# One list of steps in place of three for an mLSTM and two mixture layers on one core

## The chip, the cores and the metric

The kernel runs on one core of a Trainium2 chip. Times are device microseconds of one execution, from three runs of the kernel before; the trace comes from one further, profiled execution. Lower is better. The engines are named as in the profile: PE (TensorE), with its weight loads as PEld, DVE (VectorE), ACT (ScalarE), POOL (GpSimd) and SP (SyncE, which here only issues DMAs).

## The reference

An mLSTM recurrence over 4 batches, 8 heads, 768 positions and 40 channels feeds a dense layer with a softmax in it, and that feeds a layer in which each of the 3,072 tokens goes to one of 8 experts. Shapes: x is 3072 x 320, d_ff is 1024.

```python
for t in range(S):
    m_new = np.maximum(f_gate[:, :, t] + m, i_gate[:, :, t])
    C = f_stab * C + i_stab * outer(vt, kt); n = f_stab * n + i_stab * kt
    y[:, :, t] = sigmoid(o_gate) * (C @ qt) / np.maximum(np.abs(n . qt), 1.0)
h = x @ w_in; e = exp(h - max(h)); solu = h * e / sum(e)
x = (solu - mean) / sqrt(var + 1e-6) * g_ln @ w_out
e_idx = argmax(x @ w_gate + modality_bias[modality_id])
out[mask] = gate_w[mask, None] * (relu(x[mask] @ w1[e]) @ w2[e])
```

## The kernel before, in words

The tokens are 24 tiles of 128: tile n is batch n % 4, chunk n // 4. Work is written as small functions, here called steps, each with a tile number or the like. A list of steps in text is read by `_steps` (line 49), and `play` (line 1193) calls them in that order. Each engine has one queue, which it works through in order; what is left open is where each step's instructions stand in it. For an engine that is named to `play` the queue is the order of the list (line 1196). For the others a planner, which knows the instructions' dependencies and its own costs, lays out the queues when the program is built, and the list only says what comes first when two are free.

The steps, by what they do for a tile n:

- Loads, all on SP's queue: `load_kv` (q and k transposed, k, v; lines 261 to 270), `load_a` (line 272: the running sums of the gates, broadcast to 128 x 1024; tile "abc", three buffers), `load_ea` (line 279, three buffers), `load_sig` (line 292: 128 x 6 x 320 floats of output gates for six tiles).
- The recurrence, by chunks: `decay` (line 544, two operations on POOL) and `decay_exp` (line 553, ACT) make the decay matrix in place in "abc"; for the first four tiles `decay_mm` and `decay_exp0` do so from PE. `k_t` and `k_e` (lines 515, 522) transpose k on PE and copy it out on ACT; `score` (line 574) is q times k on PE; `pmul` (line 583, two halves on DVE) multiplies by "abc", which is its last reader but for `scale_v`. `mix_x` (line 595, PE) applies the scores and the state; `mix_e` (line 608) copies out; `mix_c` (line 615, PE and DVE) adds to the state; `scale_q`, `scale_v` and `decay_c` are POOL's. `norm_t` (line 634) transposes back on PE, `norm_d` (line 641) makes the denominator with one operation on ACT, two on DVE and one on POOL ("sig"), `norm_x` (line 650, DVE) multiplies. `k_t`, `norm_t` and `mix_c` write one and the same PSUM buffer, tag "tr", of which there is one.
- The dense layer: `xs_p`, `xs_e` (lines 661, 669) transpose x and split it; `ff_mm` (line 679, two halves of eight matmuls on PE) fills one PSUM tile "h" (one buffer); `ff_max` (DVE), `ff_exp` (ACT), `ff_u` (DVE, the last reader of "h"), `ff_sq` (ACT), `ff_r` (DVE, four small ones), `ff_y` (ACT, and a transposing DMA on SP), `ff_yl` (DVE, and another), lines 691 to 734; `proj` (line 739, 24 matmuls) and `rows` (line 750: ACT, DVE, and a DMA of the row on SP).
- Its weights: `w_raw` (line 378, a DMA on ACT's queue into one of two buffers), `w_dec` (line 384: a square on ACT, four operations on DVE), `w_in_h`, `w_in_l`, and the `wo_` steps (lines 415 to 492), which must end before `proj` 0.
- The routing: `r1a`, `r1b`, `r2`, `r3` (lines 776 to 862) for groups of 7, 7, 4, 4 and 2 tiles; `table_a`, `table_w`, `table_get`, `table_b` (lines 896 to 1007) make the lists of tokens of each expert.
- The experts, in units j of 256 or 128 tokens of one expert: `fetch_w` (line 1009: an indirect DMA on POOL's queue, 128 x 3072 floats or 128 x 2560), `fetch_x`, `stat_a` (ACT), `stat_d` (DVE), `scale` (a small matmul, then DVE), `s1h`, `s1l`, `s2h`, `s2l` (the weights split into two halves of 16 bit), `h` (line 1108, PE), `hh`, `hl`, `po` (line 1154, PE), `ob` (ACT, and an indirect DMA).

Some steps do nothing for some tiles: `mix_c` and `scale_v` for the last four, `scale_q`, `load_ea` and `decay_c` for the first four (lines 559, 567, 591, 617).

Before the change there are three lists. PROLOGUE and STEADY are played with no engine named; TAIL names ACT and SP (line 1202). PROLOGUE goes to `ff_mm` 1 and `proj` 0, STEADY to the end of the recurrence and `proj` 18, TAIL through the first units of the experts, up to `po` 2. Behind it `units` runs the other units from the lists PAIR, HALF and so on, with PE, ACT and DVE named; there are 14 units in all in this input, two of them halves.

Of the kernel before, what the change touches and what calls it, by code (L numbers as in the profile page):

```python
# [54 lines left out]
PROLOGUE = _steps("""  # L55
    gates_m 0 128, c_pad, load_kv 0, gates_a 0 128, gates_c 0 128, load_kv 1, load_kv 2, scale_q 0, k_t 0, load_kv 3,
    c_route, k_e 0, w_raw 0, decay_mm 0, score 0, load_kv 4, k_t 1, decay_exp0 0, load_sig 0, decay_mm 1,
    w_dec 0, scale_v 0, w_in_h 0, k_e 1, w_raw 1, c_row, pmul 0 0, w_dec 1, w_raw 2, decay_exp0 1, do_sig 0,
    pmul 0 1, scale_q 1, w_in_l 0, w_in_h 1, score 1, k_t 2, w_in_l 1, w_dec 2, w_in_h 2, decay_mm 2,
    scale_v 1, gates_m 128 768, gates_a 128 768, k_e 2, c_ids, gates_c 128 768, w_raw 3, w_in_l 2,  # L60
    gates_e 128 768, w_dec 3, g_close, mix_x 0, w_in_h 3, load_ea 4, load_kv 5, pmul 1 0, decay_exp0 2,
    scale_v 2, mix_c 0, wo_open, mix_e 0, norm_t 0, pmul 1 1, w_raw 4, scale_q 2, decay_c 0, k_t 3, norm_d 0,
    decay_mm 3, k_e 3, w_dec 4, score 2, w_in_l 3, decay_c 1, pmul 2 0, decay_c 2, load_a 4, load_kv 6,
    load_kv 7, norm_x 0, mix_x 1, score 3, decay_exp0 3, load_a 5, w_in_h 4, pmul 2 1, mix_c 1, mix_e 1,
    decay 4, scale_v 3, mix_x 2, norm_t 1, decay_exp 4, norm_d 1, k_t 4, decay_c 3, decay 5, load_ea 6, k_e 4,
    w_raw 5, xs_p 0, w_dec 5, scale_v 4, scale_q 3, mix_c 2, score 4, norm_x 1, w_in_h 5, w_in_l 4, pmul 3 0,
    mix_e 2, pmul 3 1, w_in_l 5, norm_t 2, mix_x 3, norm_d 2, mix_e 3, xs_e 0, k_t 5, k_e 5, w_raw 6, mix_c 3,
    score 5, load_kv 8, pmul 4 0, norm_x 2, load_kv 9, load_ea 5, scale_q 4, ff_mm 0 0, w_raw 7, decay_exp 5,
    load_sig 1, load_a 6, norm_t 3, norm_d 3, pmul 4 1, k_t 6, w_dec 6, decay 6, mix_x 4, wo_t 0, load_ea 7,
    norm_x 3, pmul 5 0, mix_e 4, k_e 6, pmul 5 1, wo_g 0, decay_exp 6, w_dec 7, wo_s 0, wo_t 1, scale_v 5,  # L70
    wo_t 2, ff_mm 0 1, ff_max 0, scale_v 6, load_a 7, scale_q 5, ff_exp 0, ff_u 0, mix_x 5, decay_c 4, wo_s 1,
    wo_g 1, w_raw 8, xs_p 1, ff_sq 0, mix_c 4, w_raw 9, ff_r 0, ff_y 0, wo_g 2, score 6, w_dec 8, decay_c 5,
    xs_e 1, wo_s 2, norm_t 4, pmul 6 0, load_kv 10, decay 7, norm_d 4, wo_t 3, scale_q 6, decay_exp 7, mix_e 5,
    k_t 7, w_dec 9, pmul 6 1, wo_g 3, norm_x 4, mix_c 5, wo_t 4, wo_s 3, k_e 7, load_a 8, w_raw 10, wo_s 4,
    wo_g 4, score 7, wo_t 5, w_dec 10, wo_g 5, wo_s 5, wo_t 6, wo_t 7, wo_s 6, wo_g 7, prep_bias, wo_g 6,
    wo_s 7, wo_m, wo_c 2, wo_c 0, load_ea 8, wo_c 3, ff_yl 0, xs_p 2, decay 8, ff_mm 1 0, norm_t 5, wo_c 1,
    wo_c 4, wo_n, ff_mm 1 1, ff_max 1, ff_exp 1, ff_u 1, ff_sq 1, wo_f 1, ff_r 1, ff_y 1, wo_f 0, wo_f 2,
    wo_close, decay_c 6, do_sig 1, load_a 9, k_t 8, k_e 8, pmul 7 0, mix_x 6, mix_e 6, mix_c 6, load_kv 11,
    norm_d 5, scale_v 7, decay_exp 8, proj 0, pmul 7 1, scale_q 7, load_ea 9, norm_x 5, xs_e 2
""")  # L80
# [1222 lines left out]
```

## Time and profile before

| | us |
|---|---|
| median of 3 runs | 716.49 |
| lowest, highest | 708.62, 721.01 |
| the profiled execution: its time, its span | 718.84, 717.0 |
| busy in the span: PE, PEld | 568.4, 434.7 |
| busy in the span: DVE, ACT, POOL | 498.5, 372.0, 359.5 |

The span goes from the first to the last instruction. A busy share is an average over all stages; matmuls overlap in the pipeline, and their ends are modelled, so that PE's share is read together with its idle time and its clock. The clock that the chip granted to PE is a share of 2.4 GHz: 1.00 is that, 0.50 is 1.2 GHz. Its mean over the span is 0.895. A wait names what ended it; the chain of waits follows from the last instruction back to what each one waited for. In the chain "issue" is time in which nothing in the profile was waited for.

### The profile page before, as it was taken

The numbers are of one execution on the slowest core, as the hardware profiler recorded it, in microseconds if no ns is written. First come the engines' busy times: TensorE is split into PE (matmuls) and PEld (weight loads), VectorE is DVE, ScalarE is ACT, GpSimd is POOL, SyncE is SP. The second block draws the span as 40 slices with busy tenths as digits, with TensorE's granted clock in tenths as the row PEclk, the third lists the DMA queues.
The fourth block names the chain that finished last, engine by engine and source line by source line (L and its number), as shares of the span: only waits on it lengthen the run. The fifth ranks groups of instructions, "written<-read, shape, count | busy, mean of one in ns | idle before, by whom it ended". The sixth has DMA issues, their size and how long they took to land.

```text
span 717.0 us, 12061 instructions
## 1 busy us (share of the span) xinstructions
PE 568.4 (79%) x4367; PEld 434.7 (61%) x4367; DVE 498.5 (70%) x1097; ACT 372.0 (52%) x570; POOL 359.5 (50%) x334
## 2 busy tenths in 40 slices
PE   3899778797987868888999555967989889988951
PEld 2777656566765656666677434735766657766740
DVE  6786564765685645546777719969788999988750
ACT  3646445744354424432534408554686787776730
POOL 3677846715452754432250322226587776756620
PEclk9999677799897989988999976979999999998976
DMA  9788695346554675533142887313257931354200
GB/s 225 201 220 229 159 166 132 100 92 167 135 167 111 114 117 129 132 85 85 41 76 48 83 247 213 73 32 84 56 107 200 258 79 42 73 157 132 68 18 3
DMA packets 126261, 87.07 MB, mean 121 GB/s; under 512 B 106415, under 2 KB 113177, under 8 KB 124904
## 3 DMA queue, kind: packets, MB, share of 16 engines
q1 hardware_dynamic: 116376, 56.38, 36.4%
q0 software_dynamic: 8224, 23.94, 11.2%
q10 hardware_dynamic: 1584, 5.77, 2.9%
q8 instruction: 43, 0.70, 0.4%
q14 instruction: 34, 0.28, 0.2%
HBM read 87.54 MB, written 9.58 MB: 135 GB/s over the span
## 4 chain that ended last, share of the span: by engine, by line
DVE 24%; PE 23%; DMA 20%; issue 12%; POOL 11%; ACT 7%; SPq 1%; POOLq 0%; DVEq 0%; ACTq 0%
PE h L688 6%; DMA stg<-in_wx,wii 5%; DMA out<-ob,idc 4%; DVE w L1098 3%; POOL abc L547 3%; PE s L580 3%; DVE w L1082 2%; DMA abc<-a_dram 2%; PE xt L601 2%; ACT w L1075 2%; POOL abc L550 2%; PE hp L1118 2%; DVE jkd L1053 2%; DMA raw<-in_w_out 2%; DMA raw<-in_w_in 2%
## 5 line engine op out<-in xcount | busy, mean ns | idle before, releaser
L1118 PE MATMUL hp<-xT,w 128*128 128x256 f16 x768 | 93.0, 281 | 5.2 <-DVE hl L1130 3.4
L1118 PEld LDWEIGHTS <-w 128*128 128x128 f16 x768 | 77.1, 102 | 17.6 <-issue 2.9
L688 PE MATMUL h<-win,xh 128*128 128x512 f32 x240 | 77.2, 445 | 2.2 <-DVE e L703 1.7
L744 PE MATMUL po<-woh,yhT 128*128 128x328 f16 x192 | 58.7, 323 | 12.0 <-DMA yhT<-yh 9.1
L1082 DVE SCALAR_TENSOR_TENSOR w<-stg,esc,w 128x1024 f16<-128x1024 f32 (+1 forms) x42 | 64.6, 1539 | 4.9 <-ACT w L1075 3.7
L1164 PE MATMUL po<-w,hl 128*128 128x320 f16 x192 | 59.0, 309 | 10.7 <-DVE hl L1130 10.7
L745 PE MATMUL po<-wol,yhT 128*128 128x328 f16 x192 | 58.6, 323 | 2.5 <-DVE wol L491 2.5
L1163 PE MATMUL po<-w,hh 128*128 128x320 f16 x192 | 59.2, 309 | 1.4 <-POOL w L1104 1.4
L1162 PE MATMUL po<-w,hh 128*128 128x320 f16 x192 | 59.3, 309 | 1.1 <-ACT hh L1126 0.6
L1075 ACT ACTIVATE w<-stg,esc 128x1024 f16<-128x1024 f32 x42 | 47.6, 1142 | 23.8 <-DVE esc L238 23.8
L569 POOL TENSOR_TENSOR qs<-qk,ea 104x512 f32<-104x512 f32 x20 | 25.9, 1296 | 62.8 <-PE xt L605 59.8
L697 ACT ACTIVATE e<-h,nm 128x1024 f32<-128x1024 f32 x24 | 26.7, 1113 | 52.8 <-DVE nm L693 52.8
L688 PEld LDWEIGHTS h<-win,xh 128*128 128x128 f32 x240 | 46.7, 208 | 11.8 <-ACT xh L672 1.8
L1170 POOL DMA_INDIRECT out<-ob,idc x26 | 34.8, 1338 | 36.7 <-ACT ob L1169 16.2
L647 POOL TENSOR_TENSOR sig<-sig,den 128x320 f32<-128x320 f32 x24 | 18.2, 756 | 68.3 <-DVE den L645 56.9
L1026 POOL DMA_INDIRECT xg<-x_dram,idc x28 | 38.4, 1370 | 23.1 <-DVE gat L1007 10.8
L688 PE MATMUL h<-win,xl 128*128 128x512 f32 x144 | 47.9, 443 | 2.3 <-DVE xl L674 2.3
L547 POOL TENSOR_TENSOR abc<-abc,gcol 128x1024 f32<-128x1024 f32 x20 | 38.8, 1939 | 21.8 <-DMA abc<-a_dram 15.8
L693 DVE TENSOR_REDUCE nm<-h 128x1 f32<-128x1024 f32 x24 | 29.3, 1222 | 27.3 <-PE h L688 27.3
L1010 POOL DMA_INDIRECT stg<-in_wx,wii x30 | 37.0, 1232 | 22.4 <-DVE lraw L755 5.4
L730 DVE SCALAR_TENSOR_TENSOR yl<-e,r_a,yh 128x1024 f16<-128x1024 f32 x24 | 34.4, 1433 | 17.5 <-ACT yh L723 17.2
L601 PE MATMUL xt<-p,va 128*41 128x128 f32 x384 | 45.6, 312 | 0.4 <-ACT den L643 0.4
(276 smaller groups left out, 1486.7 us busy)
## 6 DMA issues: line engine op xcount, KB each, us to landing
abc<-a_dram SPq DMA_DIRECT2D x20, 512.0 KB
ea<-ea_dram SPq DMA_DIRECT2D x40, 128.0 KB
qk<-in_qk SPq DMA_DIRECT2D x24, 208.0 KB
x_dram<-rowb SPq DMA_DIRECT2D x25, 192.0 KB
va<-in_kv SPq DMA_DIRECT2D x24, 164.0 KB
...
```

The source lines that it names most:

```text
L547: nc.gpsimd.tensor_tensor(out=t, in0=t, in1=gcol[:, c, b * H:(b + 1) * H].unsqueeze(2).to_broadcast([128, H, L]), op=ALU.add)
L601: nc.tensor.matmul(xt[64 * par:64 * par + VA, j, :], va[:, 4 * par + j, :], p[:, 4 * par + j, :], start=True, stop=(c == 0))
L688: nc.tensor.matmul(h[:, f, :], xx[0:kk], win[0:kk, k, f * 512:(f + 1) * 512], start=(i == 0), stop=(i == 7))
L744: nc.tensor.matmul(o, yhT[:, c, :], woh[:, c, :], start=(c == 0), stop=False)
L745: nc.tensor.matmul(o, yhT[:, c, :], wol[:, c, :], start=False, stop=False)
L1026: nc.gpsimd.indirect_dma_start(out=xg, out_offset=None, in_=x2_dram, in_offset=bass.IndirectOffsetOnAxis(ap=P2['idc'][:, 2 * j + u:2 * j + ...
L1075: nc.scalar.activation(w[:, fs], st[:, fs], AF.Copy, scale=xbuf("esc", j, [128, 2], F32)[:, 0:1])
L1082: nc.vector.scalar_tensor_tensor(out=w[r, o], in0=st[r, fs], scalar=xbuf("esc", j, [128, 2], F32)[r, 0:1], in1=w[r, fs], op0=ALU.mult, op1 ...
L1118: nc.tensor.matmul(hp[:, f, :], w[0:kk, k * FF + fc * 128:k * FF + fc * 128 + 128], xT[0:kk, xk, :], start=(i == 0), stop=(i == 7))
L1162: nc.tensor.matmul(pq[:, 0:DM], th[:, fc, us], wh, start=(fc == 0), stop=False)
L1163: nc.tensor.matmul(pq[:, 0:DM], th[:, fc, us], wl, start=False, stop=False)
L1164: nc.tensor.matmul(pq[:, 0:DM], tl[:, fc, us], wh, start=False, stop=(fc == 7))
```

## The change

The three lists become one, MAIN, with the same 1,017 steps in another order, and it is played with PE, ACT, DVE, POOL and SP named: the queue of every engine is the order of the list. The functions of the steps are the same, as are the lists behind (PAIR and the others) and what is played from them. Of the lists only the lines that the text below speaks of are shown.

```diff
-PROLOGUE = _steps("""
-    gates_m 0 128, c_pad, load_kv 0, gates_a 0 128, gates_c 0 128, load_kv 1, load_kv 2, scale_q 0, k_t 0, load_kv 3,
-    c_route, k_e 0, w_raw 0, decay_mm 0, score 0, load_kv 4, k_t 1, decay_exp0 0, load_sig 0, decay_mm 1,
-    w_dec 0, scale_v 0, w_in_h 0, k_e 1, w_raw 1, c_row, pmul 0 0, w_dec 1, w_raw 2, decay_exp0 1, do_sig 0,
-    pmul 0 1, scale_q 1, w_in_l 0, w_in_h 1, score 1, k_t 2, w_in_l 1, w_dec 2, w_in_h 2, decay_mm 2,
...
-STEADY = _steps("""
-    load_ea 10, load_kv 12, ff_mm 2 0, norm_t 6, score 8, k_t 9, load_a 10, norm_d 6, decay 9, decay_c 7,
...
-    mix_x 17, decay_c 17, pmul 18 0, load_ea 21, ff_u 12, ff_sq 12, xs_p 13, pmul 18 1, decay_exp 19, ff_r 12,
-    xs_e 13, mix_c 17, mix_e 17, proj 11, scale_q 19, load_a 21, do_sig 3, norm_t 17, norm_d 17, ff_y 12,
-    ff_mm 13 0, decay 20, k_t 20, ff_mm 13 1, load_kv 23, k_e 20, score 19, ff_yl 12, rows 11, scale_v 19,
-    ff_max 13, ff_exp 13, norm_x 17, mix_x 18, ff_u 13, scale_q 20, pmul 19 0, ff_sq 13, load_ea 22,
...
-    norm_d 18, ff_mm 14 0, ff_y 13, k_t 21, load_a 22, score 20, k_e 21, ff_mm 14 1, mix_x 19, decay 21,
...
-TAIL = _steps("""
-    ff_yl 19, r1a 2, r1b 2, r2 2, table_a 0, table_w 0, ff_mm 20 0, ff_mm 20 1, ff_max 20, ff_exp 20, a_close,
-    ff_u 20, fetch_w 0 0, r3 2, rows 18, ff_sq 20, ff_r 20, xs_p 21, table_get 0, fetch_w 0 1, stat_d 0 1,
-    fetch_w 1 1, ff_y 20, proj 19, xs_e 21, ff_mm 21 0, ff_mm 21 1, stat_a 0 1, fetch_w 1 0, stat_d 0 0,
-    table_b 0, ff_max 21, fetch_x 1, ff_exp 21, ff_u 21, ff_yl 20, fetch_x 0, stat_a 0 0, scale 0, ff_sq 21,
-    rows 19, stat_d 1 0, ff_r 21, s1h 0 2, s1h 0 1, s1h 0 0, s1l 0 1, xs_p 22, xs_e 22, ff_mm 22 0, s2h 0 1,
-    s2h 0 0, ff_mm 22 1, s1l 0 0, proj 20, stat_a 1 0, ff_y 21, ff_yl 21, ff_max 22, s2l 0 0, ff_exp 22,
-    rows 20, scale2 0, s1l 0 2, ff_u 22, xs_p 23, h 0 0, s2l 0 1, hh 0 0, ff_sq 22, stat_a 1 1, h 0 1, xs_e 23,
...
-STEPS = (PROLOGUE, STEADY, TAIL, PAIR, HALF, HALF_AHEAD, LAST_PAIR, LAST_HALF)
-    play(PROLOGUE)
-    play(STEADY)
-    play(TAIL, (engines.Activation, engines.SP))
+MAIN = _steps("""
+    c_ids, load_sig 0, w_raw 0, c_route, w_dec 0, w_raw 1, c_pad, load_kv 0, gates_m 0 128, gates_a 0 128,
+    scale_q 0, gates_c 0 128, gates_m 128 768, decay_mm 0, decay_exp0 0, w_raw 3, w_dec 1, w_in_h 1, k_t 0,
+    k_e 0, load_kv 1, gates_a 128 768, decay_mm 1, decay_exp0 1, w_raw 2, w_in_h 0, score 0, pmul 0 0,
+    scale_v 1, decay_mm 2, w_in_l 0, decay_exp0 2, pmul 0 1, mix_c 1, w_dec 2, k_t 1, w_in_l 1, mix_x 0, k_e 1,
+    scale_v 0, w_raw 4, load_kv 2, scale_v 2, w_dec 3, load_kv 3, gates_e 128 768, mix_e 0, score 1,
...
+    load_a 20, mix_e 16, mix_x 17, decay_c 3, decay_exp 19, scale_v 19, xs_e 14, score 19, k_t 21, ff_exp 13,
+    ff_u 13, proj 12, decay 20, pmul 19 0, pmul 19 1, ff_sq 13, ff_r 13, r1a 1, decay_c 21, k_e 21, load_kv 22,
+    norm_t 15, ff_y 13, rows 12, load_ea 19, ff_yl 13, load_a 21, ff_mm 14 0, mix_e 17, norm_d 15, load_ea 20,
+    ff_mm 14 1, ff_max 14, decay_exp 20, norm_x 15, score 20, mix_x 18, pmul 20 0, decay_c 23, scale_q 19,
+    ff_exp 14, ff_u 14, mix_c 18, load_kv 23, pmul 20 1, decay 21, xs_p 15, xs_e 15, proj 13, ff_sq 14,
+    ff_r 14, ff_mm 15 0, k_t 22, scale_q 20, rows 13, ff_y 14, ff_mm 15 1, mix_c 21, r1b 1, k_e 22, ff_yl 14,
+    ff_max 15, norm_t 16, score 21, mix_e 18, norm_d 16, norm_x 16, ff_exp 15, mix_x 19, decay_exp 21,
...
+    norm_d 22, proj 18, scale_q 3, xs_e 20, ff_mm 20 0, rows 18, r2 2, ff_mm 20 1, ff_sq 19, ff_r 19,
+    ff_max 20, norm_x 22, xs_p 21, xs_e 21, ff_exp 20, ff_u 20, norm_t 23, ff_y 19, ff_yl 19, r3 2, ff_mm 21 0,
+    ff_sq 20, ff_mm 21 1, ff_r 20, table_a 0, table_w 0, fetch_w 0 1, ff_max 21, norm_d 23, ff_y 20, ff_exp 21,
+    ff_yl 20, fetch_w 0 0, xs_p 22, ff_u 21, xs_e 22, norm_x 23, ff_sq 21, ff_r 21, ff_mm 22 0, table_get 0,
+    a_close, stat_a 0 1, fetch_w 1 0, r1a 3, ff_mm 22 1, ff_max 22, xs_p 23, decay_c 2, xs_e 23, mix_c 20,
+    proj 19, stat_d 0 1, stat_d 0 0, ff_exp 22, stat_a 0 0, table_b 0, scale 0, ff_y 21, ff_yl 21, fetch_x 0,
+    fetch_x 1, rows 19, s2h 0 1, s2l 0 1, scale2 0, s1h 0 2, s1l 0 2, s1h 0 0, s1h 0 1, ff_u 22, s2h 0 0,
+    s2l 0 0, proj 20, rows 20, ff_sq 22, ff_r 22, stat_a 1 0, s1l 0 1, ff_mm 23 0, fetch_w 1 1, ff_mm 23 1,
+    ff_max 23, ff_exp 23, stat_d 1 0, s1l 0 0, proj 21, stat_d 1 1, stat_a 1 1, ff_u 23, ff_y 22, scale 1,
+    scale2 1, h 0 0, hh 0 0, ff_yl 22, hl 0 0, ff_sq 23, ff_r 23, h 0 1, hh 0 1, hl 0 1, rows 21, r1b 3, h 0 3,
...
+    fetch_w 4 1, po 2 0, ob 2 0, s2h 3 1, stat_d 4 0, po 2 1, ob 2 1, s1l 3 2, fetch_w 5 0, stat_a 4 0,
+    stat_a 4 1, s2l 3 0, s2l 3 1, stat_d 4 1, scale2 3, fetch_w 5 1
+STEPS = (MAIN, PAIR, HALF, HALF_AHEAD, LAST_PAIR, LAST_HALF)
+    play(MAIN, (engines.PE, engines.Activation, engines.DVE, engines.Pool, engines.SP))
```

## Rows read from the trace of the kernel before

**Rows 1.** Stretches: length, busy time (x count) PE, PEld, DVE, ACT, POOL; clock; DMA.
```profile
0.00:70.20 70.20, 53.02 (x373) 43.87 (x375) 51.00 (x87) 36.32 (x74) 42.68 (x59) 1.00 0.85 220
70.20:149.90 79.70, 63.88 (x454) 48.48 (x455) 49.21 (x88) 43.64 (x81) 50.52 (x52) 0.76 0.58 133
149.90:406.20 256.30, 219.87 (x1804) 168.45 (x1801) 163.94 (x458) 107.57 (x181) 103.72 (x106) 0.91 0.48 107
406.20:524.90 118.70, 83.66 (x537) 59.76 (x538) 86.10 (x279) 63.32 (x85) 43.94 (x37) 0.84 0.50 114
524.90:717.00 192.10, 147.94 (x1205) 114.16 (x1203) 148.22 (x189) 121.13 (x151) 118.59 (x82) 0.92 0.41 104
```

**Rows 2.** The same view: twelve tiles, four later tiles, and one steady tile.
```profile
149.90:350.70 200.80, 167.97 (x1393) 128.81 (x1392) 120.11 (x306) 82.93 (x137) 86.78 (x86) 0.89 0.52 121
350.70:397.60 46.90, 44.43 (x373) 34.26 (x370) 35.48 (x106) 21.05 (x39) 13.24 (x17) 1.00 0.33 62
283.40:300.20 16.80, 13.89 (x119) 10.65 (x119) 8.90 (x20) 7.04 (x12) 6.79 (x6) 0.90 0.47 124
```

**Rows 3.** Chain of waits through that tile: start us, us, what.
```profile
283.46 1.28 DVE p L587 x2
...
284.79 3.80 DMA abc<-a_dram
...
288.74 1.90 POOL abc L547
...
290.69 1.97 POOL abc L550
...
292.69 1.06 ACT abc L555
...
294.34 0.73 POOL sig L647
...
295.09 0.50 DVE xn L652
```

**Rows 4.** Timeline of PE there: start, us, operation, count, [idle before <- releaser].
```profile
291.26 0.87 PE L688 MATMUL h<-win,xl 128*128 128x512 f32 x3
...
295.73 0.63 PE L519 MATMUL tk<-ident,kpad 128*128 128x128 f32 x4 [2.91 <-DVE xn L652]
...
296.95 1.48 PE L688 MATMUL h<-win,xl 128*128 128x512 f32 x3
```

**Rows 5.** Chain of waits, then waits (total, times, longest us), 400 to 450 us.
```profile
419.54 13.39 DMA stg<-in_wx,wii
...
ACT w L1049 <- DMA stg<-in_wx,wii: 17.3, 1, 17.3
...
PE po L744 <- DMA yhT<-yh: 9.1, 1, 9.1
```

**Rows 6.** Groups by line: count, busy us, mean ns, idle before; the softmax's operations.
```profile
L693 DVE TENSOR_REDUCE nm<-h 128x1 f32<-128x1024 f32 x24 | 29.3, 1222 | 27.3 <-PE h L688 27.3
...
L697 ACT ACTIVATE e<-h,nm 128x1024 f32<-128x1024 f32 x24 | 26.7, 1113 | 52.8 <-DVE nm L693 52.8
...
L703 DVE SCALAR_TENSOR_TENSOR e<-h,e 128x1024 f32<-128x1024 f32 x24 | 29.3, 1221 | 8.8 <-ACT e L697 8.4
...
L710 ACT ACTIVATE yl<-e,mu 128x1024 bf16<-128x1024 f32 x24 | 27.5, 1146 | 8.2 <-DVE e L703 8.2
L723 ACT ACTIVATE yh<-e,r_a 128x1024 f16<-128x1024 f32 x24 | 27.5, 1146 | 35.5 <-DVE r_a L238 35.5
```

**Rows 7.** Chain of waits, 0 to 150 us, and the group of the weights' squares.
```profile
0.81 5.14 DMA raw<-in_w_in
...
93.30 11.33 DMA raw<-in_w_out
...
L393 ACT ACTIVATE s<-raw 128x512 f32<-128x512 f32 x11 | 7.4, 676 | 9.5 <-DMA raw<-in_w_in 4.8 <-DMA raw<-in_w_out 4.7
```

**Rows 8.** Line 730, 150 to 410 us: duration ns least/median/most, first and last start.
```profile
L730 DVE SCALAR_TENSOR_TENSOR yl<-e,r_a,yh x17: 1277/1285/2222, 156.0 to 404.0; 128x1024 f16<-128x1024 f32 x17
```

More of the change, by code (lines that the diff above doesn't have):

```diff
@@ L51, in _steps @@
     return [(name, *map(int, args)) for name, *args in steps]
-PROLOGUE = _steps("""
-    gates_m 0 128, c_pad, load_kv 0, gates_a 0 128, gates_c 0 128, load_kv 1, load_kv 2, scale_q 0, k_t 0, load_kv 3,
-    c_route, k_e 0, w_raw 0, decay_mm 0, score 0, load_kv 4, k_t 1, decay_exp0 0, load_sig 0, decay_mm 1,
-    w_dec 0, scale_v 0, w_in_h 0, k_e 1, w_raw 1, c_row, pmul 0 0, w_dec 1, w_raw 2, decay_exp0 1, do_sig 0,
-    pmul 0 1, scale_q 1, w_in_l 0, w_in_h 1, score 1, k_t 2, w_in_l 1, w_dec 2, w_in_h 2, decay_mm 2,
[L60 to L79, printed above, removed]
@@ L136 @@
-""")
-TAIL = _steps("""
-    ff_yl 19, r1a 2, r1b 2, r2 2, table_a 0, table_w 0, ff_mm 20 0, ff_mm 20 1, ff_max 20, ff_exp 20, a_close,
-    ff_u 20, fetch_w 0 0, r3 2, rows 18, ff_sq 20, ff_r 20, xs_p 21, table_get 0, fetch_w 0 1, stat_d 0 1,
-    fetch_w 1 1, ff_y 20, proj 19, xs_e 21, ff_mm 21 0, ff_mm 21 1, stat_a 0 1, fetch_w 1 0, stat_d 0 0,
-    table_b 0, ff_max 21, fetch_x 1, ff_exp 21, ff_u 21, ff_yl 20, fetch_x 0, stat_a 0 0, scale 0, ff_sq 21,
-    rows 19, stat_d 1 0, ff_r 21, s1h 0 2, s1h 0 1, s1h 0 0, s1l 0 1, xs_p 22, xs_e 22, ff_mm 22 0, s2h 0 1,
-    s2h 0 0, ff_mm 22 1, s1l 0 0, proj 20, stat_a 1 0, ff_y 21, ff_yl 21, ff_max 22, s2l 0 0, ff_exp 22,
-    rows 20, scale2 0, s1l 0 2, ff_u 22, xs_p 23, h 0 0, s2l 0 1, hh 0 0, ff_sq 22, stat_a 1 1, h 0 1, xs_e 23,
-    stat_d 1 1, hh 0 1, proj 21, ff_r 22, ff_y 22, rows 21, scale 1, r1a 3, r1b 3, r2 3, table_a 1, table_w 1,
-    fetch_w 2 0, h 0 2, hl 0 0, hl 0 1, r3 3, ff_mm 23 0, ff_mm 23 1, fetch_w 2 1, h 0 3, ff_max 23,
-    table_get 1, ff_exp 23, s1h 1 0, ff_yl 22, hh 0 2, s1l 1 0, hh 0 3, s1h 1 1, hl 0 2, proj 22, s1l 1 1,
-    scale2 1, ff_u 23, table_b 1, hl 0 3, ff_sq 23, s2h 1 0, ff_r 23, ff_y 23, s2l 1 0, s1h 1 2, s1l 1 2,
-    rows 22, po 0 0, h 1 0, stat_a 2 0, fetch_w 3 0, s2h 1 1, hh 1 0, stat_d 2 0, stat_a 2 1, po 0 1, ff_yl 23,
-    stat_d 2 1, fetch_x 2, ob 0 1, scale 2, hl 1 0, s1h 2 1, s1h 2 0, r1a 4, scale2 2, h 1 1, hh 1 1, proj 23,
-    s2l 1 1, s1h 2 2, hl 1 1, rows 23, fetch_w 3 1, ob 0 0, s1l 2 0, h 1 2, hh 1 2, s2h 2 0, r1b 4, s1l 2 1,
-    r2 4, table_a 2, s2l 2 0, hl 1 2, h 1 3, hh 1 3, s1l 2 2, r3 4, hl 1 3, stat_a 3 1, stat_a 3 0, table_w 2,
-    po 1 0, stat_d 3 0, po 1 1, ob 1 0, s2h 2 1, s2l 2 1, h 2 0, fetch_x 3, hh 2 0, ob 1 1, fetch_w 4 1, h 2 3,
-    stat_d 3 1, scale 3, hl 2 0, table_get 2, s1h 3 1, h 2 1, hh 2 1, hl 2 1, s1h 3 0, s2h 3 1, h 2 2,
-    fetch_w 4 0, hh 2 3, hh 2 2, table_b 2, s1h 3 2, hl 2 2, stat_a 4 0, s1l 3 0, stat_a 4 1, s1l 3 1, s1l 3 2,
-    stat_d 4 0, hl 2 3, fetch_w 5 0, stat_d 4 1, scale2 3, po 2 0, po 2 1, s2h 3 0, s2l 3 1, ob 2 0, ob 2 1,
-    fetch_x 4, s2l 3 0, fetch_w 5 1
```

122 lines of the change are left out of this document (73 added, 49 removed).

## The prediction

> **What bounds the kernel now.** I read the stretches first, cut at ends of row maxima and projections [rows 1]. Up to 524.9 us the three lists run; from there to 717.0 the unchanged loop of pairs (192.1 us). In the three lists TensorE is idle 17.2, 15.8, 36.4 and 35.0 us in the four stretches (length less busy), 104 in all, and its granted clock falls from 1.00 to 0.76, 0.91 and 0.84. So PE is the busiest engine, but not full; in the fourth stretch VectorE is (86.10 of 118.70).
>
> Then the third stretch, where one tile follows another. Of its 200.8 us up to 350.7 (12 tiles, 16.7 us each) PE works 167.97 at clock 0.89; one tile looked at alone has 16.80 us, 13.89 of PE at 0.90, and only 8.90, 7.04 and 6.79 of DVE, ACT and POOL [rows 2]. No engine is full. The chain of waits through that tile shows why [rows 3]: `pmul` 17 frees the buffer for `load_a` 20 (1.28, then a DMA of 3.80), POOL's two `decay` operations follow (1.90, 1.97), `decay_exp` 20 (1.06), and behind it on ACT, by order alone, `norm_d` 15; then POOL's `sig` 0.73, `norm_x` 0.50, and only then `k_t` 19 on PE, as it needs the one PSUM buffer "tr" that `norm_x` empties. After `k_t` stand the second half of `ff_mm`, `score` 18 and `pmul` 18, which frees the next buffer: a ring, 16.8 us long. PE's own rows show what the ring costs [rows 4]: 2.91 us idle before `k_t`, and three matmuls of the same kind that took 0.87 us before the gap take 1.48 after it: the lower of the two clocks (1.2 against 2.4 GHz). With mean clock 0.90, a tile's 13.89 us hold 16.80 x 0.10 = 1.7 us of lost clock; at the full one the tile is 12.2 us of PE.
>
> Last the fourth stretch [rows 5]: of four weight fetches in a row one puts 13.39 us of DMA on the chain, ACT stands 17.3 us in `stat_a`, and PE 9.1 us before `proj` 19, whose transposed input shares the DMA engines with them.
>
> **The change part by part.** No instruction is added or removed; the steps are the same set. Every cost is one of order.
>
> *One list for three, five engines fixed.* The switches themselves cost nothing: each engine has always run its own queue in order, and no operation is issued for them. What could cost is that an engine no longer gets past a step that is late. I price that by place.
>
> *The ring.* The new list has `norm_t` 15, `load_a` 21, `ff_mm` 14 0, `mix_e` 17, `norm_d` 15, `ff_mm` 14 1, `decay_exp` 20, `norm_x` 15, `score` 20, `mix_x` 18, `mix_c` 18. Two links go: `norm_d` stands ahead of `decay_exp` on ACT, and the next user of "tr" (`mix_c`) has a whole `ff_mm`, a `score` and a `mix_x` before it on PE, which cover the about 2 us of `norm_d`, `sig` and `norm_x` [rows 3]. `load_a` 21 needs the buffer of tile 18, whose `pmul` is a tile back, so SP does not stand there; it moves behind two transposes and a row write on SP's queue, and its 3.80 + 3.87 + 1.06 us are covered by more than a tile of PE work before `pmul` 21 (without that cover they would be the ring again). What is late next is the softmax: `ff_max`, `ff_exp`, `ff_u`, `ff_sq`, `ff_y` [rows 6], 1.22, 1.11, 1.22, 1.15 and 1.15 us, then `k_e` 22 on ACT, for which `norm_t` 16 waits. PE has a tile less a transpose between `ff_mm` 14 1 and that `norm_t`, about 12 us. In between ACT also waits for `xs_p` 15 and for `proj` 13 (`rows` 13), so by PE's own order I put `k_e` at about 11 us: a margin of some 1.4 us, an estimate from these rows. So PE nearly fills. I leave 15 of the 36.4 us idle (r1, r2, r3 of the routing on DVE and POOL and one sigmoid come once each): -21. A fuller PE holds its clock, as the four tiles from 350.7 on do, with 44.43 of 46.90 us busy at clock 1.00 [rows 2]; 0.91 to 0.96 on 219.87 us of work is -11.5. Together -33. Ends: -56 (no idle, clock 1.00) and +10 (each old wait replaced, and a few more).
>
> *The start.* The new list issues `c_ids` and the 960 KB `load_sig` 0 on SP ahead of `load_kv` 0. With the list of ids (193 KB) that is 1.15 MB, at the 220 GB/s of the first stretch [rows 1] 5.2 us of transfers ahead of the first tile; bounds 0 and +5.2. `w_raw` 1 goes behind the square of `w_dec` 0 on ACT, while the gates and `decay_mm` stand behind the same `w_dec` 0 on DVE. I take +4, nearer the upper end, since the first raw weights took 5.14 us even alone [rows 7]. The row shows DMA engines 85% busy there. The Trainium skill (its title page "Trainium Kernel Development and Optimization", section Key Constraints) says that DMAs of the SP, ACT and POOL queues run on the same 16 engines and interleave. By that the weights on ACT's queue would not stand behind the sigmoid's bytes but share with them, the price would be about half, and the sum would be 678.
>
> *70 to 150 us.* The weights of the output projection, `wo_*`, spread over the first four tiles. Now one raw load stands 11.33 us on the chain, and ACT stood 9.5 us in all before the eleven squares [rows 7]. The new list issues later loads just ahead of their use; it has less PE work before each `ff_mm`. Ends -11 (that wait goes) and +28 (ACT stands half of 5.14 us in each of eleven). I take 0, nearest to the 9.5 that it stands already.
>
> *406 to 525 us.* The fetches go from four in a row to two, one and one, with `ff_mm` 22, `proj` 19 and 20 and `ff_mm` 23 between; `proj` 19 moves behind `ff_mm` 22, so that its transposes have two tiles to land. `stat_a` 0 1 still stands ahead of `ff_exp` 22 on ACT, a tile after its fetch: I estimate 5 of the 17.3 us there. DVE sets the floor, 86.10 us [rows 1]; `h` 0 0 now stands behind `scale` 1, which needs all four fetches. I take a third of the 32.6 us above that floor: -10; ends -27 and 0.
>
> *The loop of pairs* is entered with the same steps done: 0.
>
> Sum against the profiled run: 718.8 + 4 + 0 - 33 - 10 + 0 = 679.8; that run is 2.3 us above the median of 716.49, well inside the shown spread. Forecast **680 us**.
>
> **The rivals.**
>
> *Give-back (about the same).* The ring goes, but the strict order makes ACT wait for raw weights in the prologue: eleven times half of 5.14, +28: 708. For: ACT now waits for DMAs ahead of `k_e` and `mix_e` in that text, and DMA is 85% busy there. Against: only 9.5 us were waited so far with the same two buffers. To this side also belongs that the order on the engines hardly changes, since each queue was fixed before too: 717. Against that: `norm_d` after `decay_exp` is a fact of the old trace and is reversed in the new text.
>
> *Slower: the softmax ring.* If `k_e` comes later than its margin, `norm_t` holds PE in every tile, and the lower clock returns. A tile then has 12.2 + 1.7 + s us. It is worse than the old 16.7 from s = 2.8 us on, so if ACT and DVE bring `k_e` 1.4 + 2.8 = 4.2 us later than I reckon; with s = 4.5 it is 18.4, times 17 tiles +29, with the start +4: 752. For: seven steps of two engines in one row, each with a hop between. Against: DVE has 8.90 and ACT 7.04 us of work in a tile, so neither is full.
>
> *Everything gained.* No idle in the third stretch and its clock full, -56, and -16 in the fourth: 647. Against: the one-off routing steps. POOL's operations can hold DVE's: `ff_yl` takes 1.28 us at the least and 2.22 at the most in the steady part [rows 8], and more POOL work falls beside it here. The Trainium skill ("SBUF — State Buffer", section "SBUF: two separate sides") says that the two share a port pair by an exclusive lock, held for a whole instruction, against DVE operations with two SBUF inputs. The longest case is in line with that. By that rule in full, waiting for both `decay` operations, DVE has 8.90 + 3.87 = 12.8 us a tile, more than PE's 12.2, and this rival would end about 10 us later, at 657.
>
> **How the numbers follow.** Forecast 0.56, everything gained 0.10, give-back or no effect 0.22, softmax ring 0.12. The forecast's own range is 652 to 702: the prologue's terms with -11 and +20, the third stretch's -33 with 12 either way, the tail's with 10, not all at once. Eight in ten reach over most of the give-back: 650 to 716. Over 2% (about 14 us, what a measurement tells from no change) means below 702 or above 731: faster 0.66, within 0.22, slower 0.12.
>
> **What would show it.** In the new trace: no idle of 3 us before `k_t`, and the chain of waits through a steady tile made of PE rows, not of `load_a` and `decay`; ff tiles 13 us apart with clock 0.95 or more; the first score and first row maximum some 4 us late for their work; `proj` 19 without a DMA wait; `stat_a` 0 1 waiting 5 us. It is wrong if PE waits for `k_e` or `mix_c` in each tile, if ACT's waits for raw weights grow past 20 us, or if `scale` 1 holds PE before `h` 0 0 for longer than twice the old 9.1 us wait before `proj` 19.

## The result, and the profile after

The changed kernel took **675.28 us** (median of four runs, 671.24 to 681.57), beside 717.27 for the kernel before: a ratio of **0.943** (95% interval 0.929 to 0.958). The forecast was 680. Two later sets of runs, on other occasions, gave 674.3 (ratio 0.946, 0.928 to 0.965) and 678.5 (0.947, 0.941 to 0.954).

The stretches of the profiled run (671.24 us, span 669.4), cut at the same steps as [rows 1]; the third goes from the row maximum of tile 3 to that of tile 20. Columns as there:

```profile
0.00:69.70 69.70, 47.10 (x280) 38.48 (x280) 49.73 (x77) 30.47 (x65) 34.66 (x52) 0.85 0.68 176
69.70:136.90 67.20, 57.67 (x460) 47.24 (x461) 45.11 (x79) 35.75 (x74) 44.79 (x43) 0.82 0.54 136
136.90:362.10 225.20, 206.15 (x1884) 160.52 (x1881) 178.42 (x450) 120.43 (x197) 113.59 (x116) 1.00 0.66 143
362.10:480.40 118.30, 84.59 (x541) 62.19 (x542) 95.20 (x303) 63.98 (x84) 51.37 (x43) 0.88 0.66 120
480.40:669.40 189.00, 145.49 (x1207) 114.02 (x1205) 145.92 (x192) 122.61 (x151) 118.34 (x82) 0.93 0.38 103
```

Against [rows 1] the five differ by -0.5, -12.5, -31.1, -0.4 and -3.1, together -47.6 us. Some matmuls of `mix_x` and `mix_c` that once stood before the 149.9 mark now stand behind 136.9, so the third stretch does a little more work in less time. That is where most of the gain is: PE is idle 19.0 us there instead of 36.4, and busy 206.2 instead of 219.9. The groups of PE's instructions show how. First the kernel before, 149.9 to 406.2 us (busy us, mean ns of one, idle time just before them and what ended it):

```profile
L688 PE MATMUL h<-win,xh 128*128 128x512 f32 x170 | 53.6, 438 | 1.5 <-DVE e L703 1.0 <-ACT xh L672 0.5
L519 PE MATMUL tk<-ident,kpad 128*128 128x128 f32 x52 | 9.8, 320 | 28.8 <-DVE xn L652 15.2 <-issue 7.1 <-DVE rt L809 3.1
```

Then the changed one, 136.9 to 362.1 us:

```profile
L683 PE MATMUL h<-win,xh 128*128 128x512 f32 x170 | 47.4, 408 | 0.1
L514 PE MATMUL tk<-ident,kpad 128*128 128x128 f32 x52 | 8.2, 280 | 0.8 <-PE dc L619 0.8
```

The idle time before `k_t`, 28.8 of the 36.4 us that PE stood in that stretch, is 0.8. Part of it stands elsewhere now: 6.3 us before `mix_c` (0.7 before the change) and 5.6 before `norm_t` (4.3). And the same 170 matmuls of `ff_mm` take 408 ns each where they took 438: the granted clock is 1.00 instead of 0.91. In two more profiles of the changed kernel (a1 and c4 below) the same stretch took 228.2 and 233.0 us, both at clock 0.96.

The waits of the helper engines there (total, times, longest us), before and after:

```profile
ACT abc L555 <- POOL abc L550: 27.2, 10, 5.8
POOL abc L547 <- DMA abc<-a_dram: 11.6, 6, 4.5
DVE xn L652 <- POOL sig L647: 11.4, 11, 3.7
```

```profile
POOL abc L542 <- DMA abc<-a_dram: 15.5, 5, 4.3
DVE xn L647 <- POOL sig L642: 8.5, 10, 1.7
ACT abc L550 <- POOL abc L545: 1.0, 1, 1.0
```

ACT stood 27.2 us in `decay_exp` before, and 1.0 us now; POOL's own wait for the loads did not fall (11.6, 15.5). The traces show the order: before, `load_a` 20 was issued 0.1 us after `pmul` 17 had freed its buffer, and `decay_exp` 20 ended 39 us before `pmul` 20 began (293.8, 333.0). Now `load_a` 20 is issued 10.8 us after `pmul` 17, and `decay_exp` 20 ends 6 us before its use.

### The profile page after: what moved, and what is told of

Same layout as the page of the kernel before. It is cut to its first block, busy times and chain, and to the rows that moved or that the text cites. A ratio compares the mean times of both kernels' runs of the same rounds, so it can differ in the third digit from the quotient of the medians.

```text
span 669.4 us, 12026 instructions
## 1 busy us (share of the span) xinstructions
PE 541.0 (81%) x4367; PEld 422.5 (63%) x4367; DVE 514.4 (77%) x1097; ACT 373.2 (56%) x570; POOL 362.8 (54%) x334
## 4 chain that ended last, share of the span: by engine, by line
PE 33%; DVE 25%; DMA 14%; ACT 11%; issue 9%; POOL 5%; DVEq 0%; ACTq 0%; POOLq 0%
PE h L683 7%; DMA out<-ob,idc 5%; DMA stg<-in_wx,wii 4%; DVE w L1077 4%; ACT w L1070 3%; PE hp L1113 3%; PE xt L596 3%; PE s L575 2%; DMA raw<-in_w_out 2%; PE dp L529 2%; DVE w L1093 2%; DVE jkd L1048 2%; PE xt L600 2%; DVE yl L725 2%; PE po L739 2%
## 5 line engine op out<-in xcount | busy, mean ns | idle before, releaser
L683 PE MATMUL h<-win,xh 128*128 128x512 f32 x240 | 73.1, 438 | 7.1 <-DVE e L698 6.4
L739 PE MATMUL po<-woh,yhT 128*128 128x328 f16 x192 | 55.4, 309 | 4.9 <-DVE rowb L753 3.0
L683 PEld LDWEIGHTS h<-win,xh 128*128 128x128 f32 x240 | 47.1, 207 | 18.9 <-issue 6.4
L1158 PE MATMUL po<-w,hh 128*128 128x320 f16 x192 | 57.4, 299 | 1.7 <-POOL w L1099 1.6
L1157 PE MATMUL po<-w,hh 128*128 128x320 f16 x192 | 57.5, 300 | 0.1
L740 PE MATMUL po<-wol,yhT 128*128 128x328 f16 x192 | 55.3, 308 | 0.0
L1165 POOL DMA_INDIRECT out<-ob,idc x26 | 37.1, 1427 | 30.9 <-ACT ob L1164 16.0
L852 POOL DMA_INDIRECT ids_dram<-tokid,pi x24 | 24.9, 1039 | 38.2 <-DVE tb L909 29.3
L1044 ACT ACTIVATE jka<-stg 128x2048 bf16<-128x2048 f32 (+1 forms) x24 | 40.7, 1694 | 7.0 <-DMA stg<-in_wx,wii 6.7
L683 PE MATMUL h<-win,xl 128*128 128x512 f32 x144 | 44.4, 419 | 0.1
L596 PE MATMUL xt<-p,va 128*41 128x128 f32 x384 | 40.8, 304 | 1.9 <-DVE p L582 1.7
L725 DVE SCALAR_TENSOR_TENSOR yl<-e,r_a,yh 128x1024 f16<-128x1024 f32 x24 | 37.3, 1555 | 5.8 <-ACT yh L718 5.8
```

Of the source, the lines that this page charges most:

```text
L596: nc.tensor.matmul(xt[64 * par:64 * par + VA, j, :], va[:, 4 * par + j, :], p[:, 4 * par + j, :], start=True, stop=(c == 0))
L683: nc.tensor.matmul(h[:, f, :], xx[0:kk], win[0:kk, k, f * 512:(f + 1) * 512], start=(i == 0), stop=(i == 7))
L725: nc.vector.scalar_tensor_tensor(out=yl, in0=u_t.pop(n), scalar=r_a[:, n:n + 1], in1=yh, op0=ALU.mult, op1=ALU.subtract)
L739: nc.tensor.matmul(o, yhT[:, c, :], woh[:, c, :], start=(c == 0), stop=False)
L740: nc.tensor.matmul(o, yhT[:, c, :], wol[:, c, :], start=False, stop=False)
L1044: nc.scalar.activation(jk[0], st[:, 0:hw], AF.Square, accum_out=wsq[:, q, 0:1])
```

## The experiments

**All engines free: the new text with the planner (a2).**

```diff
-    play(MAIN, (engines.PE, engines.Activation, engines.DVE, engines.Pool, engines.SP))
+    play(MAIN)
```

> The new list, with no engine named in play(), so that the planner orders each engine's steps from the same text. Theory (the ring is the order of decay_exp and norm_d on ACT): the planner pulls decay_exp ahead of norm_d again, the ring partly returns, 700 to 715 us, with idle of PE before k_t in the steady tiles and clock dips there. Rival (the text of the list does it, not its strictness): 672 to 682 us and no idle there.

Measured: 713.7 us, ratio 1.000 (0.994 to 1.006). The text alone gains nothing. Waits in its third stretch (137 to 405 us):

```profile
POOL abc L542 <- DMA abc<-a_dram: 48.5, 10, 8.2
ACT abc L550 <- POOL abc L545: 43.6, 11, 8.5
DVE xn L647 <- POOL sig L642: 32.8, 16, 6.9
```

The planner puts a chunk's `load_a`, `decay` and `decay_exp` in early, POOL and ACT stand in them, and `sig` and `norm_x` come late. The idle that was expected before `k_t` came elsewhere on PE (`mix_c`, `xs_p`, `mix_x`), so this half of the expectation was wrong.

The changed kernel beside it (a1):

> The changed kernel itself, beside its variants. Every theory: 675 us (671 to 682), ratio to the kernel before about 0.943.

It took 674.3 us, as every theory had it.

**The old lists with ACT's order turned round (a3).** ACT alone follows the list from `k_t` 12 on, and so runs `norm_d` ahead of `decay_exp`.

```diff
-    play(STEADY)
+    at = STEADY.index(('k_t', 12))
+    play(STEADY[:at])
+    play(STEADY[at:], (engines.Activation,))
```

> The kernel before with its three lists, ACT alone held to the list from k_t 12 on: norm_d comes ahead of decay_exp there, all other engines stay with the planner. Theory (the ACT link of the ring is what costs): eight to ten tiles lose 2 to 3 us each, 687 us (680 to 700); the tiles before k_t 12 stay at 16 to 17 us. Rival (the single PSUM buffer and the other engines' order hold the ring as well): 712 to 720 us.

Measured: 727.2 us, ratio 1.024 (1.000 to 1.048): no gain. But the two halves of the stretch tell different things; first `ff_max` 10 to 16, then `ff_max` 16 to 20:

```profile
266.00:344.00 78.00, 73.51 (x676) 56.47 (x672) 53.59 (x154) 42.42 (x69) 33.05 (x30) 1.00 0.49 111
344.00:410.00 66.00, 47.90 (x304) 34.05 (x299) 33.66 (x126) 20.43 (x37) 14.84 (x17) 0.84 0.21 45
```

Six tiles took 78.4 us (13.1 each, clock 1.00) where they had taken 97.8, so the ring was open. The load of "abc" still left as soon as its buffer came free (`pmul` 17, `load_a` 20, `sig` 15, `decay` 20):

```profile
271.14 0.68 DVE L587 TENSOR_TENSOR p<-s,abc 128x512 f32<-128x512 f32 x1
271.88 0.34 SPq L275 DMA_DIRECT2D abc<-a_dram  x1
274.96 0.72 POOL L647 TENSOR_TENSOR sig<-sig,den 128x320 f32<-128x320 f32 x1 [4.30 <-DVE den L645]
276.66 1.90 POOL L547 TENSOR_TENSOR abc<-abc,gcol 128x1024 f32<-128x1024 f32 x1 [0.97 <-DMA abc<-a_dram]
```

What had changed is what stands behind it: `sig` 15 came ahead of `decay` 20 on POOL, and `decay_exp` 20 ran only at 296.15, where before it had stood ahead of `norm_d` 15. In the second part 41.8 us had become 66.0, with 18 us of idle. The planner had laid the other queues out anew. On POOL it set seven small indirect DMAs of `r3` ahead of the `sig` of tile 20:

```profile
341.67 1.04 POOL L857 DMA_INDIRECT ids_dram<-tokid,pi  x1 [7.50 <-DVE den L645]
...
349.40 0.97 POOL L857 DMA_INDIRECT ids_dram<-tokid,pi  x1 [0.30 <-issue]
350.37 0.76 POOL L647 TENSOR_TENSOR sig<-sig,den 128x320 f32<-128x320 f32 x1
```

PE stood 5.96 us before `k_t` for it. Opening one link of an order that is planned as a whole moves the stop.

**The ACT link alone put back into the new list (a4).** For ten tiles `decay_exp` m goes directly ahead of `norm_d` m-5, as it was before:

```diff
# m = 20
-    ff_mm 14 0, mix_e 17, norm_d 15, load_ea 20, ff_mm 14 1, ff_max 14, decay_exp 20,
+    ff_mm 14 0, mix_e 17, decay_exp 20, norm_d 15, load_ea 20, ff_mm 14 1, ff_max 14,
```

> The changed kernel with one link of the ring put back: in ten tiles decay_exp stands directly ahead of norm_d on ACT again. Theory of the prediction (two links were cut, the other user of the tr buffer stands a ff_mm, a score and a mix_x behind, and load_a does not wait for its buffer): half cover is left, 675 to 686 us, and PE waits at most 1 us more per tile. Rival (the ACT order alone is the ring): 16.8 us per tile again in ten tiles, about 710 us.

Measured: 670.7 us, ratio 0.941 (0.923 to 0.960). The rival (710) is out. ACT's wait for "abc" is 2.0 us in all: the `decay` was long done, and an early `decay_exp` that waits for nothing costs nothing. The order of the two steps, on which the prediction had put the ring, is not enough by itself.

**PE alone held to the list (b1), and PE alone free (b2).**

```diff
-    play(MAIN, (engines.PE, engines.Activation, engines.DVE, engines.Pool, engines.SP))
+    play(MAIN, (engines.PE,))
```

> The new list with PE alone held to it; ACT, DVE, POOL and SP ordered by the planner. Theory after the first four runs (either link that is cut opens the ring, and PE's own order cuts the one through the tr buffer): 670 to 685 us, tiles of 13 to 14 us at clock 1.00. Rival (the helpers' order is needed too, since with all free POOL and DVE were late for norm_x, up to 6.9 us at once): 695 to 715 us, PE waiting for xn, kT and xs in the third stretch as in the run with all engines free.

Measured: 729.4 us, ratio 1.012 (1.002 to 1.021), beside 723.9 for the kernel before in this group of runs (b1 to b4); POOL waited 40.9 us for the loads of "abc" and ACT 41.8 us for POOL. The waits are the rival's, the time lies beyond its 715: a fixed PE over late helpers is no better than the old order.

```diff
-    play(MAIN, (engines.PE, engines.Activation, engines.DVE, engines.Pool, engines.SP))
+    play(MAIN, (engines.Activation, engines.DVE, engines.Pool, engines.SP))
```

> The new list with ACT, DVE, POOL and SP held to it and PE alone ordered by the planner. Theory (PE's order counts): 685 to 710 us, with idle of PE before k_t or norm_t in the third stretch. Rival (the four others' order leaves the planner hardly a choice on PE): 670 to 680 us.

Measured: 686.7 us, ratio 0.947 (0.930 to 0.965), with 233.0 us in the third stretch and no wait of ACT for "abc". The time lies in the theory's range, but the idle before `k_t` that it asked for (0.3 us) does not come; the ratio is that of the changed kernel. So the gain sits in the order of the four helpers; PE's own adds nothing that can be told.

**The early chain put back into the new list (c1, c2)**, all five engines fixed. For tiles 12 to 23 `load_a` m goes directly behind the last step that frees its buffer, and `decay` m (in the first kernel `decay_exp` m too) directly ahead of the next `norm_d`. This bunches them: three `decay` stand in a row ahead of `norm_d` 10, two ahead of `norm_d` 12 and of 14, where the steady tiles of the kernel before had one each.

```diff
# m = 20, the second kernel (c2)
-    pmul 17 1, ... norm_t 14, norm_d 14, ... load_a 20, mix_e 16, ... decay 20, ... decay_exp 20,
+    pmul 17 1, load_a 20, ... norm_t 14, decay 20, norm_d 14, ... mix_e 16, ... decay_exp 20,
# the first kernel (c1)
+    pmul 17 1, load_a 20, ... norm_t 14, decay 20, decay_exp 20, norm_d 14, ... mix_e 16,
```

> The changed kernel, all five engines still fixed, with the decay chain made early again for tiles 12 to 23: load_a m directly behind the last step that frees its buffer (pmul or scale_v of m-3), decay m and decay_exp m directly ahead of the next norm_d. Theory after eight runs (what the old order cost is ACT standing in decay_exp for a load that was only just issued, with norm_d and k_e behind it: ACT waited 27.2 us for abc in the kernel before, 43.6 and 41.8 us in the two runs that gained nothing, 1 to 2 us in those that gained): ACT waits 25 us or more for abc again, PE idles before k_t, norm_t or mix_c, 695 to 720 us. Rival (PE's own new order covers it, as in a4): 671 to 682 us, no new idle of PE.

> As c1, but decay_exp stays where the new list has it, so that only SP and POOL are early; and, far from it at the start, c_ids and load_sig 0 are moved behind load_kv 3. Theory (ACT's order is the costly link; in a3 early loads and decays with a late decay_exp gave 13.0 us per tile): 670 to 682 us. Rival (sig stands behind decay on POOL in the same way): 690 to 710 us, DVE waiting over 20 us for sig. At the start, by the reason of my prediction (the sigmoid's and the list's bytes ahead of the first tile) the first score ends 3 to 4 us earlier than 22.8; by the rival (score 0 stands behind the whole of decay_mm 1 on PE) it stays within 0.5 us.

Measured on one chip, with the changed kernel at 678.5 beside them:

> The changed kernel once more, beside c3 on one chip: 675 us (671 to 682) by every theory.

| | us | ratio to before | third stretch |
|---|---|---|---|
| changed kernel (c4) | 678.5 | 0.947 (0.941 to 0.954) | 233.0 |
| c2: `load_a`, `decay` early | 696.1 | 0.969 (0.963 to 0.976) | 251.1 |
| c1: `decay_exp` early too | 710.4 | 0.986 (0.980 to 0.992) | 261.4 |

With all three steps early, 31.8 of the 42.6 us that the change gained on that chip (721.17 less 678.53) are gone again. On ACT of that kernel one sees the wait from inside:

```profile
266.47 1.06 ACT L544 ACTIVATE abc<-abc 128x1024 f32<-128x1024 f32 x1 [5.83 <-POOL abc L539]
269.50 1.06 ACT L544 ACTIVATE abc<-abc 128x1024 f32<-128x1024 f32 x1 [1.97 <-POOL abc L539]
270.46 0.16 ACT L632 ACTIVATE den<-tr 128x8 f32<-128x8 f32 x1
270.51 0.59 ACT L599 ACTIVATE xs<-xt 128x512 f32<-128x512 f32 x1
```

Two `decay_exp` wait for their data, `norm_d` and `mix_e` (0.59 us of work) stand behind them by order alone, and PE's next row is `mix_x` with 7.85 us of idle before it. Its waits in the third stretch (136 to 397 us):

```profile
DVE den L633 <- ACT den L632: 34.6, 5, 13.7
ACT abc L544 <- POOL abc L539: 30.7, 11, 5.8
PE xt L590 <- ACT xs L599: 16.2, 2, 8.4
PE trx L654 <- DVE xn L641: 10.4, 4, 5.1
```

ACT's 30.7 us are what the theory asked for; PE's idle is before `mix_x` and `xs_p`, which it did not name. Where only SP and POOL are early (c2), the rival of its expectation holds, in time and in sign: `norm_x` on DVE waits 22.7 us for `sig`, against 6.8 to 8.5 in the three profiles of the changed kernel. Waits from 137 to 388 us, then two rows of POOL:

```profile
DVE xn L642 <- POOL sig L637: 22.7, 12, 5.9
POOL abc L537 <- DMA abc<-a_dram: 14.4, 4, 7.3
PE trx L655 <- DVE xn L642: 8.4, 4, 3.3
```

```profile
265.55 1.09 POOL L540 TENSOR_SCALAR_AFFINE_SELECT abc<-abc 128x1024 f32<-128x1024 f32 x1
266.61 0.72 POOL L637 TENSOR_TENSOR sig<-sig,den 128x320 f32<-128x320 f32 x1
```

`sig` follows `decay` without a gap. POOL's wait for the loads (14.4) is no longer than in the changed kernel (15.5 to 17.3): what holds `sig` up is the work ahead of it in the queue. So there are two links, in these bunched orders of 17.5 and 14.3 us by the medians (18.1 and 10.3 in the third stretch): `sig` behind `decay` on POOL, and `norm_d` and `mix_e` behind `decay_exp` on ACT. Where ACT's link holds, POOL's does not show: in c1 `norm_x` waits 6.9 us for `sig`. At the start c2 has `c_ids` and `load_sig` 0 behind `load_kv` 3, and the first score ended at 22.6 instead of 22.8, so that the reason given for the start is wrong.

**The tail.** Two single edits to the changed kernel:

```diff
# b3: fetch_w 1 1 ahead of both fetch_x on POOL's queue
-    fetch_w 1 0, r1a 3, ... ff_mm 23 0, fetch_w 1 1, ff_mm 23 1,
+    fetch_w 1 0, fetch_w 1 1, r1a 3, ... ff_mm 23 0, ff_mm 23 1,
# b4: the scale of the second unit behind h of the first
-    stat_d 1 1, stat_a 1 1, ff_u 23, ff_y 22, scale 1, scale2 1, h 0 0, ... r1b 3,
+    ff_u 23, ff_y 22, h 0 0, ... stat_d 1 1, stat_a 1 1, scale 1, scale2 1, r1b 3,
```

> The changed kernel with fetch_w 1 1 directly behind fetch_w 1 0, ahead of both fetch_x on POOL's queue. Theory (scale 1 waits 8.8 us on PE for the fourth weight fetch, which stands behind fetch_x, which waits 8.4 us for the table): -5 to -9 us, about 667, and the wait before scale 1 under 3 us. Rival (DVE, 95 of 118 us busy in that stretch, or the x fetch now later, takes the time back): 672 to 677 us, a new wait of PE for DVE or xg before h 0 0.

> The changed kernel with stat_d, stat_a, scale and scale2 of 1 1 moved behind h 0 0 and h 0 1, so that PE does not stand before h for the fourth fetch. Theory (that wait was on the path): -5 to -9 us, about 667. Rival (scale 1 is needed soon after anyway, by r1b, or the wait moves to s1 of the second expert): 672 to 677 us.

Measured: 674.3 us, ratio 0.935 (0.926 to 0.944), and 685.0 us, ratio 0.951 (0.932 to 0.970). Both intervals overlap that of the changed kernel, which was not run beside them. By the profiles, from `ff_max` 20 to the end the first has 302.5 us and the second 309.6, the changed kernel 304.9 to 307.0 in its three. So at most some 2 to 5 us came from the first, and none from the second. In the first the wait before `scale` 1 is 1.5 us, but 8.8 us was that of one profile only: in the two others of the changed kernel it is 2.1 and 5.2. The waits of PE in the first:

```profile
PE pi L994 <- DVE idg L991: 6.2, 1, 6.2
PE h L677 <- DVE e L692: 5.4, 2, 3.8
PE pw L1048 <- DVE w L1042: 1.5, 1, 1.5
```

The first of these is `table_b`, whose copy ("idg") stands on DVE behind two `stat_d` that wait for the weights. Therefore a last kernel (c3) moved it ahead, together with the rest that stood behind a fetch, and `score` 0 ahead of `decay_mm` 1 at the start:

```diff
-    k_e 0, load_kv 1, gates_a 128 768, decay_mm 1, decay_exp0 1, w_raw 2, w_in_h 0, score 0,
+    k_e 0, load_kv 1, gates_a 128 768, score 0, decay_mm 1, decay_exp0 1, w_raw 2, w_in_h 0,
...
-    stat_a 0 1, fetch_w 1 0, ... proj 19, stat_d 0 1, stat_d 0 0, ff_exp 22, stat_a 0 0, table_b 0, scale 0,
-    ff_y 21, ff_yl 21, fetch_x 0, fetch_x 1, ... fetch_w 1 1,
+    fetch_w 1 0, fetch_w 1 1, ... proj 19, table_b 0, fetch_x 0, fetch_x 1, stat_d 0 1, stat_d 0 0,
+    ff_exp 22, stat_a 0 1, stat_a 0 0, scale 0, ff_y 21, ff_yl 21,
```

> The changed kernel with score 0 ahead of decay_mm 1, and in the tail table_b 0 and both fetch_x ahead of the squares of the first weights (stat_d 0 1, stat_d 0 0, stat_a 0 1 now behind ff_exp 22), fetch_w 1 1 directly behind fetch_w 1 0. Theory (in the tail PE waits for steps that stand by order alone behind a weight fetch of 13 to 15 us: table_b behind stat_d on DVE, ff_mm 22 behind stat_a 0 1 on ACT, scale 1 behind fetch_x): first score 3 to 4 us earlier, the tail 4 to 8 us shorter, 664 us (659 to 669). Rival (DVE, 95 of 118 us busy there, gives it back, as the two single edits b3 and b4 showed no gain): 671 to 677 us, the tail not shorter.

Measured: 688.6 us, ratio 0.958 (0.952 to 0.964), 10 us slower than the changed kernel on the same chip. Neither part gained:

```profile
DVE idg L992 <- DMA idg<-ids_dram,tb: 9.3, 1, 9.3
PE pi L995 <- DVE idg L992: 8.4, 1, 8.4
```

`table_b` now waits for its own gather, with DVE standing in it. From `ff_max` 20 to the end this kernel has 305.5 us, the changed one beside it 304.9, so the tail is neither shorter nor longer, and the loss lies ahead of it. At the start `score` 0 did not come earlier, so that `decay_mm` 1, the reason of c2's rival, is not what holds it alone, while the first `ff_max` came 6.8 us later (76.5 against 69.7); at `ff_max` 20 the kernel was 6.6 us behind. No kernel here is shown to be faster than the changed one.

## Why the prediction was right, and where it was not

**The sum.** The forecast of 680 is close to the 675.28, and in part by luck: the terms were +4, 0, -33, -10 and 0, the first profile has -0.5, -12.5, -31.1, -0.4 and -3.1. The second and the fourth are off by 12.5 and 9.6 us in opposite directions. The third, which rests on the account of the ring, came as forecast.

**The ring: right in size and place.** Expected were -33 us, -21 of idle and -11.5 of clock; the first profile has -31.1, with 17.4 us less idle and 13.7 less busy, and the two others -28.1 and -23.3. No idle to speak of is left before `k_t`, tiles are 13.2 us apart in the first profile, and the clock is 1.00, 0.96 and 0.96 (forecast 0.96). The step that gave the cause named two links: `norm_d` behind `decay_exp` on ACT, and the next user of "tr" without cover on PE. The first is what held the kernel before, as the row of `sig` in the tile of [rows 3] shows:

```profile
294.34 0.72 POOL L647 TENSOR_TENSOR sig<-sig,den 128x320 f32<-128x320 f32 x1 [1.68 <-DVE den L645]
```

POOL had finished `decay` and stood 1.68 us for "den", which needs ACT's `norm_d`; in 15 of the 17 times in that stretch POOL stood idle for DVE before `sig`. But the link counts only where the data are late: a4 put `decay_exp` ahead of `norm_d` again, behind a `decay` long done, for no loss. And a second one lies under it, which the prediction did not see: with ACT's link gone, `sig` of that tile could have come at most 1.68 us sooner, and then the order on POOL, `decay` ahead of `sig`, would have held it. That order costs by itself in c2; in a3, where six tiles ran without the ring, the planner had turned it round as well. The second link that the prediction named, cover on PE, is not what gains: b1 kept PE's order and gained nothing, b2 let it go and kept the gain. That the load now goes out later, behind other work on SP's queue, was called covered; no kernel moved the load alone, but a3 had 13.1 us per tile with loads issued at once, so that the later load is not shown to help.

**The list and its strictness.** That the switches cost nothing stands. The rival that the order hardly changes is out: the same text without the five names (a2) gives 1.000, so the names, which make the queues follow the list, are what changes the order.

**The softmax ring** did not come. PE waited 4.3 us in five places for `k_e`, longest 1.9, so the margin put at 1.4 us was about used up, in a few tiles.

**The start: the number right for the score, its reason wrong, and without effect.** The first score ended 3.9 us later (22.8 against 18.9), forecast +4. By c2 the bytes of `load_sig` 0 and the id list are not the cause, so neither of the two prices, nor the 678 that the rule of the Trainium skill ("Trainium Kernel Development and Optimization", section Key Constraints) would have made of it, has anything to weigh. (The 5.14 us of the first raw weights, taken to be those of a load alone, had six loads of SP's queue beside them, issued from 0.81 to 3.84.) PE of c3, then ACT of the changed kernel:

```profile
21.04 2.08 PE L570 MATMUL s<-qk,kT 40*128 40x128 f32 x16 [5.01 <-ACT kT L514]
```

```profile
19.86 0.63 ACT L400 ACTIVATE win<-w 128x512 fp32r<-128x512 f32 x1 [2.13 <-DVE w L395]
20.40 0.58 ACT L519 ACTIVATE kT<-tk 128x512 f32<-128x512 f32 x1
```

`k_e` 0 runs at 20.40 (before: 14.41), behind `w_in_h` 1, which waits for DVE. That is read from the traces; no kernel moved `k_e` 0. By the first `ff_max` nothing was left of it (69.7 against 70.2).

**70 to 150 us: forecast 0, measured -12.5**, beyond the lower end (-11). The reason given for that end, that the 11.33 us wait for raw weights [rows 7] goes, did not come: it is now two of 7.43 and 7.47 on the chain, and ACT stands 7.6 us before the squares instead of 9.5. PE is idle 9.5 us there instead of 15.8 and busy 57.7 instead of 63.9, with 460 matmuls instead of 454. Which order brought that stays open; no kernel took this stretch alone.

**The tail: this term failed.** Forecast -10, measured -0.4. The step that failed is DVE's floor, held at 86.10 us: DVE is busy 95.2 of 118.3 us, with 303 operations in the stretch instead of 279. The time above the floor did fall by about the third that was taken, from 32.6 to 23.1 us, and the floor rose by 9.1. `proj` 19 no longer waits for a DMA, as forecast, but PE waits elsewhere (PE, 375 to 416 us, then the fetches in the chain of waits):

```profile
375.49 2.47 PE L683 MATMUL h<-win,xh 128*128 128x512 f32 x5 [3.85 <-DVE e L698]
...
387.99 0.40 PE L1000 MATMUL pi<-ident,idg 4*128 4x4 f32 x2 [3.44 <-DVE idg L997]
...
413.38 0.59 PE L1054 MATMUL pw<-wsq,onef 128*128 128x4 f32 x2 [8.78 <-ACT w L1044]
```

```profile
374.94 11.61 DMA stg<-in_wx,wii
...
395.41 16.32 DMA stg<-in_wx,wii
```

At `ff_max` 22 the kernel was 64 us ahead of the old one, at the first `h` 34.2. The fourth fetch goes out only at 395.41, as it stands on POOL behind `fetch_x`, which waits 8.4 us for the table. The prediction had noted that `h` 0 0 stands behind `scale` 1, but did not ask when that last fetch is issued. Yet that wait alone was not worth much: in b3 the fourth fetch leaves 17.7 us after `ff_max` 20 instead of 33.0 to 36.3, and the first `h` starts 48.2 us after it, against 47.8 to 51.4 in the three profiles of the changed kernel.

**DVE and POOL.** `ff_yl` in the third stretch took 1,604 ns in the mean in the first profile (1,481 before), but 1,406 and 1,428 in the two others; at most 2,764, 2,262 and 2,256 (2,222 in [rows 8]). So a rise is not shown. The longest cases are in line with the rule of the Trainium skill ("SBUF — State Buffer", section "SBUF: two separate sides"), but the 12.8 us per tile by that rule in full did not become the bound: DVE was busy 178.42 us over 17 tiles, 10.5 each.
